# Windowed attention and two MLPs: sixteen attention items with the exponential taken after the transpose and a turned value product, and zero products on TensorE

## The chip, the cores and the metric

One NeuronCore of a Trainium2 chip runs the whole program as one launch. The metric is the device time of that core in microseconds (us), median over runs. TensorE is PE in the profile's rows, VectorE DVE, ScalarE ACT, GpSimd POOL; SP issues the DMAs.

## What is computed

Attention over 4 batches, 8 heads, 576 positions and head size 64, with a window of 128 keys and a linear bias per head, then two MLPs (512 to 2048 to 512) on the 2304 tokens. The weights arrive as 8-byte floats. Cut to what matters:

```python
scores = scale * q @ k.T + bias          # bias = -slope[h] * |i - j|
scores = where((rel >= 0) & (rel < 128), scores, -1e9)
attn = exp(scores - max(scores))
attn = attn / (sum(attn) + 1e-09)
x = (attn @ v)                           # heads side by side: 2304 x 512
h = x @ w_in;  x = (max(h, 0) + alpha * min(h, 0)) @ w_out
h = x @ moe2_w_in;  out = (h * sigmoid(1.702 * h)) @ moe2_w_out
```

## The kernel before

An attention *item* is one (unit, batch, head). Unit 0 holds queries 0 to 255, unit 1 queries 256 to 575; there are 64 items, unit 0 first. The first 16 (`n < FP`: batches 0 and 1 of unit 0) work in plain float32; the later ones split every operand into two float32r halves. Only the first 16 change.

Such a float32 item goes through these stages, each a function that is called with the item's number: `a_qk` (TensorE, L342: scores of two chunks, 128 and 256 keys), `a_bias` (VectorE, L362: scores plus bias, negated, into `tt`, and the row minimum into `st`), `a_exp` (ScalarE, L378: two exponentials in place with the row sum, each with a read of its accumulator), `a_recip` (VectorE, L386 and L387), `a_norm` (VectorE, L398, two), `a_trans` (TensorE, L411: three 128x128 transposes into PSUM), `a_pt_hi` (ScalarE, L418: copy of 384 columns into `pt`), `a_av` (TensorE, L432: the padded values `vz` as weights, `pt` streaming 256 and 128 columns; two heads share one tile `x`), and for each odd head `a_x3` (ScalarE L479 and VectorE L107: `xh` and `xl`, the two halves of the first MLP's input). GpSimd lays the values into `vz` (L328).

Ten *rounds* of a preamble (L741 to L776) run items 0 to 9 and decode weights beside them; then come the steps of the first MLP. A step is one of 16 slices `f` of the hidden size for one block `k` of 256 tokens: `m1_h` (L493, 12 products), `m1_n` (ScalarE L508), `m1_g` (VectorE L518, ScalarE L522), `m1_lo` (VectorE), and two steps later `m1_o` (L544, 12 products). Two steps carry one attention item. Block 0 needs items 0 to 7, and its 16 steps also decode the rest of the 32 chunks of the first MLP's weights. Each 512 KB chunk takes `w_scale` (ScalarE L147 and L150), `w_shift` and `w_add` (VectorE L154 and L159) and `w_split` (ScalarE L102, VectorE L107; for two early chunks VectorE L103). At most four chunks are in flight (`wstage`).

A scheduler sets the order of each engine's queue before the launch; engines then take their queue strictly in that order. The decode's instructions are pinned in program order, the others move. PSUM tiles of attention share four buffers (`ps_a`); the first MLP's accumulators are `o0` and `o1`.

Of the kernel before, what the change touches and what calls it, by code (L numbers as in the profile page):

```python
# [21 lines left out]
P = 128  # L22
# [43 lines left out]
def tile_window_attention__then__two_mlps(  # L66
# [255 lines left out]
    @stage  # L322
    def a_split_v(n, b, u, h, U):
        nv = (2, 4)[u]
        vr = raw_of(n)[:, UCOLS[u] - nv * D : UCOLS[u]].rearrange("p (j d) -> p j d", d=D)
        if n < FP:
            d0 = (h % 2) * D
            nc.gpsimd.tensor_copy(vzs[n % 2][:, :, d0 : d0 + D], vr)  # L328
# [43 lines left out]

    @stage
    def a_exp(n, b, u, h, U):
        tt, s = tts[n % 2], sts[n % 2]
        for i, (c0, rows, kk, keys) in enumerate(U["chunks"]):
            t = tt[:rows, i * 256 : i * 256 + keys]
            nc.scalar.activation(  # L378
                t, t, AF.Exp, bias=s[:rows, i : i + 1], scale=-1.0, accum_out=s[:rows, 4 + i : 5 + i]
            )  # L380

    @stage
    def a_recip(n, b, u, h, U):
        s = sts[n % 2]
        m = len(U["chunks"])
        nc.vector.tensor_scalar(s[:, 8 : 8 + m], s[:, 4 : 4 + m], 1e-9, None, op0=ALU.add)  # L386
        nc.vector.reciprocal(s[:, 12 : 12 + m], s[:, 8 : 8 + m])  # L387

    @stage
    def a_norm(n, b, u, h, U, eng):  # L390
        tt, s = tts[n % 2], sts[n % 2]
        for i, (c0, rows, kk, keys) in enumerate(U["chunks"]):
# [8 lines left out]
    def a_trans(n, b, u, h, U):  # L401
        tt = tts[n % 2]
        banks = [ps_a.tile([P, 512], F32, tag="a", name="pt") for _ in range(1 + u)]
        for i, (c0, rows, kk, keys) in enumerate(U["chunks"]):
# [9 lines left out]
    @stage  # L414
    def a_pt_hi(n, b, u, h, U, i):
        if i <= u:
            x, c, w = st["t", n][i]
            nc.scalar.copy(pts[n % 2] if n < FP else ar["pth"][:, c : c + w], x[:, :w])  # L418

# [5 lines left out]

    @stage
    def a_av(n, b, u, h, U):
# [40 lines left out]
    def a_x3(n, b, u, h, U):  # L468
# [3 lines left out]
        if n < FP:  # L472
            xp = st["x", n]
        t = u * B * UNITS[0]["nq"] + b * nq
# [232 lines left out]
    for t in vzs:  # L707
        nc.gpsimd.memset(t, 0.0)
    for t in sts:
# [26 lines left out]
    for t in tts:  # L736
        nc.gpsimd.memset(t[:, 512:768], 0.0)
    W1 = 2 * NF
    a_qk(0)
    w_ahead()  # L740
    for n in range(H + 2):  # L741

        if n == 4:
            nc.sync.dma_start(out=relt, in_=rel)
            nc.sync.dma_start(out=alph, in_=alpha)
            nc.gpsimd.tensor_scalar(beta, alph, -1.0, 1.0, op0=ALU.mult, op1=ALU.add)
        a_av(n - 2)
        a_split_v(n)
# [29 lines left out]
    a_split(n)  # L778
    for i in range(2):
        a_pt_lo(n - 2, i)  # L780
    a_recip(n - 1)
    a_norm(n - 1, "dve")
    a_av(n - 2)
    a_x1(n - 2)
    a_x2(n - 2)
    a_x3(n - 2)
    at0.close()
# [4 lines left out]
    for s, (k, f) in enumerate(steps):  # L792
# [14 lines left out]
        m1_h(k, f)  # L807
        if s % 2 == 0:
            a_trans(m)
            a_qk(n)  # L810
            a_pt_hi(m, 0)
            m1_n(k, f)
            m1_g(k, f)
            a_pt_hi(m, 1)
            a_bias(n)
            wd("shift")
            a_pt_lo(m, 0)
# [6 lines left out]
        else:  # L824
            a_av(m)
            if n == FP:
                a_parts()
# [11 lines left out]
            m1_lo(k, f, "dve")  # L839
            a_x3(n - 1)  # L840
        if k == 0:
# [136 lines left out]
```

## Time and profile before

| what | value |
|---|---|
| time, median of 3 runs | 948.61 us (948.21 to 950.05) |
| the profiled execution's own time | 951.22 us |
| its span, first to last instruction | 949.4 us |
| busy: PE, DVE, ACT | 926.7, 687.6, 526.7 us |

A row of groups names line, engine, operation, tiles, shape and count, then busy time and the mean of one; a row of the timeline gives start, length and engine, and how long the engine was idle before it and for what. A matmul's shown length contains its latency; the pitch of a stream is the distance of two starts. "x4" for two float32 products is right: each runs as two instructions.

### The profile page before, as it was taken

The numbers are of one execution on the slowest core, as the hardware profiler recorded it, in microseconds if no ns is written. First come the engines' busy times: TensorE is split into PE (matmuls) and PEld (weight loads), VectorE is DVE, ScalarE is ACT, GpSimd is POOL, SyncE is SP. The second block draws the span as 40 slices with busy tenths as digits, with TensorE's granted clock in tenths as the row PEclk, the third lists the DMA queues.
The fourth block names the chain that finished last, engine by engine and source line by source line (L and its number), as shares of the span: only waits on it lengthen the run. The fifth ranks groups of instructions, "written<-read, shape, count | busy, mean of one in ns | idle before, by whom it ended". The sixth has DMA issues, their size and how long they took to land.

```text
span 949.4 us, 17872 instructions
## 1 busy us (share of the span) xinstructions
PE 926.7 (98%) x6536; PEld 862.2 (91%) x6536; DVE 687.6 (72%) x1743; ACT 526.7 (55%) x1325; POOL 89.7 (9%) x127
## 2 busy tenths in 40 slices
PE   6899999999999999999999999999999999999997
PEld 3698899999999999999988888888898899999997
DVE  6898876778888888888457753685333798878876
ACT  5999866667667676676344443564232553433333
POOL 1100211122222222222000000000000000000000
PEclk9999999999999999999999999999999999999999
DMA  9666511223222222221023344665332333433323
GB/s 242 205 217 209 183 54 55 66 68 91 69 67 91 67 68 91 67 90 44 1 89 110 112 128 169 203 227 199 117 124 99 134 134 117 151 133 132 132 72 112
DMA packets 44041, 112.45 MB, mean 118 GB/s; under 512 B 5041, under 2 KB 15153, under 8 KB 43953
## 3 DMA queue, kind: packets, MB, share of 16 engines
q1 hardware_dynamic: 43952, 111.31, 36.1%
q8 instruction: 51, 0.84, 0.4%
q14 instruction: 38, 0.30, 0.1%
HBM read 82.98 MB, written 28.31 MB: 117 GB/s over the span
## 4 chain that ended last, share of the span: by engine, by line
PE 91%; DVE 2%; issue 1%; ACT 0%; DVEq 0%; ACTq 0%
PE h L493 21%; PE h L591 21%; PE p L658 18%; PE o L544 17%; PE p L544 5%; PE x L444 3%; PE pt L411 3%; PE s L351 1%; PE s L352 1%; PE s L342 1%; DVE wl L107 0%; DVE wd L159 0%; ACT oh L102 0%; PE x L432 0%; DVE wd L154 0%
## 5 line engine op out<-in xcount | busy, mean ns | idle before, releaser
L493 PE MATMUL h<-xh,wh 128*128 128x256 f32 (+1 forms) x512 | 151.9, 298 | 1.4 <-ACT xh L479 1.4
L493 PE MATMUL h<-xh,wl 128*128 128x256 f32 (+1 forms) x512 | 152.3, 298 | 0.0
L493 PE MATMUL h<-xl,wh 128*128 128x256 f32 (+1 forms) x512 | 151.4, 296 | 0.0
L658 PE MATMUL p<-wh,oh 128*128 128x256 f32 x504 | 136.3, 284 | 1.0 <-ACT oh L102 0.6
L658 PE MATMUL p<-wl,oh 128*128 128x256 f32 x504 | 136.2, 283 | 0.0
L544 PE MATMUL o<-gh,wl 128*128 128x256 f32 x448 | 127.5, 286 | 0.0
L544 PE MATMUL o<-gh,wh 128*128 128x256 f32 x448 | 125.9, 286 | 0.7 <-ACT gh L522 0.7
L544 PE MATMUL o<-gl,wh 128*128 128x256 f32 x448 | 125.5, 281 | 1.1 <-DVE gl L107 1.1
L658 PE MATMUL p<-wh,ol 128*128 128x256 f32 x504 | 119.2, 283 | 0.4 <-DVE ol L107 0.4
L591 PE MATMUL h<-x2h,wh 128*128 128x512 f32 (+1 forms) x320 | 117.9, 368 | 0.0
L591 PE MATMUL h<-x2l,wh 128*128 128x512 f32 (+1 forms) x320 | 117.8, 368 | 0.0
L591 PE MATMUL h<-x2h,wl 128*128 128x512 f32 (+1 forms) x320 | 117.7, 368 | 0.0
L605 DVE TENSOR_TENSOR g<-h,sg 128x512 f32<-128x512 f32 (+1 forms) x80 | 51.0, 638 | 90.7 <-ACT sg L601 90.5
L601 ACT ACTIVATE sg<-h 128x512 f32<-128x512 f32 (+1 forms) x80 | 44.4, 555 | 108.5 <-PE h L591 108.3
L493 PEld LDWEIGHTS h<-xh,wh 128*128 128x128 f32 x512 | 96.3, 189 | 5.2 <-ACT xh L479 1.9
L493 PEld LDWEIGHTS h<-xh,wl 128*128 128x128 f32 x512 | 96.6, 189 | 3.9 <-DVE wl L107 0.6
L493 PEld LDWEIGHTS h<-xl,wh 128*128 128x128 f32 x512 | 97.0, 189 | 3.0 <-issue 0.3
L658 PEld LDWEIGHTS p<-wh,oh 128*128 128x128 f32 x504 | 96.5, 192 | 2.1 <-ACT oh L102 2.0
L658 PEld LDWEIGHTS p<-wl,oh 128*128 128x128 f32 x504 | 96.7, 192 | 0.1
L518 DVE SCALAR_TENSOR_TENSOR g<-n,beta,h 128x256 f32<-128x256 f32 x112 | 53.2, 475 | 54.1 <-ACT n L508 53.8
L508 ACT ACTIVATE n<-h 128x256 f32<-128x256 f32 x112 | 42.8, 383 | 87.8 <-PE h L493 87.3
L658 PEld LDWEIGHTS p<-wh,ol 128*128 128x128 f32 x504 | 86.5, 192 | 0.7 <-DVE ol L107 0.6
(105 smaller groups left out, 2203.0 us busy)
## 6 DMA issues: line engine op xcount, KB each, us to landing
ws<-in_w_in_dram SPq DMA_DIRECT2D x32, 512.0 KB, 3.9
ws<-in_w_out_dram SPq DMA_DIRECT2D x32, 512.0 KB, 3.7
raw<-in_u_dram SPq DMA_DIRECT2D x32, 512.0 KB, 3.5
g2d<-g SPq DMA_DIRECT2D x32, 512.0 KB, 3.1
gr<-g2d SPq DMA_DIRECT2D x32, 512.0 KB, 3.2
raw<-in_u_dram SPq DMA_DIRECT2D x16, 320.0 KB, 2.8
wd<-x2d SPq DMA_DIRECT2D x36, 128.0 KB, 2.9
out_dram<-ob SPq DMA_DIRECT2D x16, 256.0 KB, 3.4
```

The costliest lines, as they stand in the source:

```text
L342: nc.tensor.matmul(o[:, :keys], raw[:, c0 : c0 + rows], raw[:, 256 + kk : 256 + kk + keys], start=True, stop=True)
L351: nc.tensor.matmul(o[:, :n_], q, kh[:, ks : ks + n_], start=True, stop=False)
L411: nc.tensor.transpose(banks[bank][:, dst : dst + P], src, ident)
L444: nc.tensor.matmul(x[:, oc : oc + nq], v, p[:, col : col + nq], start=(i == 0 and k == 0), stop=(i == len(js) - 1 and k == 1), skip_group_ ...
L493: nc.tensor.matmul(ph, w[:, 0, c * P : (c + 1) * P], x[:, c, r : r + n], start=(c == 0 and i == 0), stop=(c == NC - 1 and i == 2),)
L508: nc.scalar.activation(n, ph, AF.Relu, scale=-1.0)
L518: nc.vector.scalar_tensor_tensor(g, n, beta[:, f : f + 1], ph, op0=ALU.mult, op1=ALU.add)
L544: nc.tensor.matmul(o, w[:, 1, c * P : (c + 1) * P], g, start=(f == 0 and (k == KM or c % 2 == 0) and i == 0), stop=(f == NF - 1 and i == 2 ...
L591: nc.tensor.matmul(ph[:, :n], w[:, f % 2, c * P : (c + 1) * P], x[:, c, :n], start=(c == 0 and i == 0), stop=(c == NC - 1 and i == 2),)
L601: nc.scalar.activation(sg[:, :n], ph[:, :n], AF.Sigmoid, scale=1.702)
L605: nc.vector.tensor_tensor(g[:, f % 2, :n], ph[:, :n], sg[:, :n], op=ALU.mult)
L658: nc.tensor.matmul(o[:, m, :], g[:, a, m * P : (m + 1) * P], w, start=(p == 0 and m == 0 and i == 0), stop=(p == NF // 2 - 1 and i == 2), ...
```

## The change

For items 0 to 15 the exponential, its row sum and the division move. `f_sub` turns `tt` into score minus maximum (chunk 0 on VectorE, chunk 1 on ScalarE). `a_trans` then transposes those differences, and `f_exp` takes one exponential of 384 columns from PSUM into `pt`, where the plain copy was. `f_av` turns the product round: 128 columns of `pt` are the weights and the values stream, 64 columns and a column of ones, which yields the row sum; three products of 65 columns instead of two of 256 and 128. `f_div` divides once for two heads (three VectorE instructions), and `a_x3` transposes the result back (two transposes for two heads). `a_exp`, `a_recip`, `a_norm`, `a_pt_hi` and `a_av` do nothing for these items any more. An item's tail runs a round earlier (`a_x3(n - 1)` for `a_x3(n - 2)`).

From round 2 on each preamble round issues five products of a zero tile by itself (bfloat16, 128x128 by 128x512) into `o1`, three after `f_av` and two after the transposes: 40 in all. Their result is overwritten later.

```diff
-    vzs = [apf.tile([P, 2, P], F32, name=f"vz{i}") for i in range(2)]
+    vzs = [apf.tile([P, 2, D + 1], F32, name=f"vz{i}") for i in range(2)]
+    xq = apf.tile([P, 2, 2, D], F32, name="xq")
...
+    def f_sub(n, b, u, h, U):
...
+            if i:
+                nc.scalar.activation(t, t, AF.Identity, bias=s[:rows, i : i + 1], scale=-1.0)
+            else:
+                nc.vector.tensor_scalar(t, t, s[:rows, i : i + 1], -1.0, op0=ALU.subtract, op1=ALU.mult)
...
+    def f_exp(n, b, u, h, U):
+        if n < FP:
+            x, c, w = st["t", n][0]
+            nc.scalar.activation(pts[n % 2], x[:, :w], AF.Exp)
...
+    def f_av(n, b, u, h, U):
...
+        for c, j, col in ((0, 0, 0), (1, 0, 128), (1, 1, 256)):
+            nc.tensor.matmul(
+                x[:, c, h % 2, : D + 1], pt[:, col : col + P], vz[:, j, :],
+                start=(c == j == h % 2 == 0), stop=(c == j), skip_group_check=True,
+            )
...
+    def f_div(n, b, u, h, U):
...
+        nc.vector.tensor_scalar(r, x[:, :, :, D], 1e-9, None, op0=ALU.add)
+        nc.vector.reciprocal(f, r)
+        nc.vector.tensor_tensor(xq, x[:, :, :, :D], f.unsqueeze(3).to_broadcast([P, 2, 2, D]), op=ALU.mult)
...
     def a_av(n, b, u, h, U):
         if n < FP:
-            x = st["x", n] = st["x", n - 1] if h % 2 else ps_a.tile([P, 512], F32, tag="a", name="x")
-            pt, vz = pts[n % 2], vzs[n % 2]
-            for j in range(2):
-                nc.tensor.matmul(
-                    x[:, j * P : 256], vz[:, j, :], pt[:, j * 256 : 256 + j * P],
-                    start=(h % 2 == 0 and j == 0), stop=(h % 2 == 1 and j == 1), skip_group_check=True,
-                )
             return
...
         if n < FP:
-            xp = st["x", n]
+            xp = ps_a.tile([P, 512], F32, tag="a", name="x")
+            for i in range(2):
+                nc.tensor.transpose(xp[:, i * P : (i + 1) * P], xq[:, i, :, :], ident)
...
+    idle = pso.tile([P, 2, T1], F32, tag="o1", name="idle")
+    zero = tts[0][:, 512:768].bitcast(BF16)
+
+    def busy(m):
+        for _ in range(m):
+            tc.keep_in_program_order(nc.tensor.matmul(idle, zero[:, :P], zero, start=True, stop=True))
...
-        a_av(n - 2)
+        f_exp(n - 1)
         a_split_v(n)
...
         a_bias(n)
+        f_sub(n)
         w("split")
-        a_exp(n)
-        a_recip(n - 1)
+        f_av(n - 1)
+        busy(3 if n > 1 else 0)
         w("shift")
-        a_norm(n - 1, "dve")
-        a_trans(n - 1)
         w("add")
         w_ahead()
+        f_div(n - 1)
+        a_trans(n, True)
+        busy(2 if n > 1 else 0)
         w("scale")
-        a_x3(n - 2)
         if n % 4 == 0:
             w("split")
             w("shift")
-        a_pt_hi(n - 1, 0)
-        a_pt_hi(n - 1, 1)
+        a_x3(n - 1)
```

TensorE's queue in the preamble, before, from the scores of item 4 on (`h` is a first piece of `m1_h`):

```order
L342 MATMUL s<-raw_144 128x128
L342 MATMUL s<-raw_144 128x256
L432 MATMUL x<-pt_161,vz_159 128x256
L432 MATMUL x<-pt_161,vz_159 128x128
L411 MATMUL pt<-ident,tt_146 128x128 x3
L493 MATMUL h<-xh,wh_223 128x256
L493 MATMUL h<-xh,wh_286 128x256
```

The same place after the change; the last two rows come three times in a row there, and twice more behind the next transposes. Ahead of this piece stand the turned product of item 1 and five such products:

```order
L518 MATMUL x<-ident,xq 128x128 x2
L342 MATMUL s<-raw_144 128x128
L342 MATMUL s<-raw_144 128x256
L461 MATMUL xq<-vz_158,pt_161 128x65 x3
L789 LDWEIGHTS tt_146
L789 MATMUL idle<-tt_146 128x512
```

The transposes back (L518) stand in front of the scores of item 4, so these wait for the division of items 0 and 1; the turned product of item 2 stands right behind the scores.

ScalarE's queue around the exponential of item 3, before:

```order
L418 COPY pt_161<-pt 128x384
L378 ACTIVATE tt_147,st_149<-tt_147,st_149 128x128
L378 ACTIVATE tt_147,st_149<-tt_147,st_149 128x256
L147 ACTIVATE wd<-ws 128x512
L150 ACTIVATE ws<-ws 128x512
L479 CAST xh<-x 128x256
```

And after:

```order
L389 ACTIVATE pt_161<-pt 128x384
L381 ACTIVATE tt_147<-tt_147,st_149 128x256
L147 ACTIVATE wd<-ws 128x512
L150 ACTIVATE ws<-ws 128x512
L524 CAST xh<-x 128x256
L381 ACTIVATE tt_146<-tt_146,st_148 128x256
```

Two exponentials with a sum have become one subtraction, the copy has become the exponential, and the decode of a chunk stands between them as before. Up to the first `n` of block 0, 13 chunks are scaled on ScalarE and 11 items have their bias on VectorE in either order; up to the 24th `g` it is all 32 chunks and 22 items in either.

## Rows read from the trace of the kernel before

**Rows 1.** The page's second part: 40 slices of 23.7 us, busy tenths and granted clock.
```profile
PE   6899999999999999999999999999999999999997
...
PEclk9999999999999999999999999999999999999999
```

**Rows 2.** Windows: stretch, length; busy (count) of PE, PEld, DVE, ACT, POOL; clock; DMA.
```profile
0.00:49.00 49.00, 35.99 (x135) 25.04 (x136) 35.70 (x126) 35.70 (x92) 7.22 (x24) 1.00 0.81 227
49.00:107.00 58.00, 55.43 (x410) 50.03 (x410) 53.81 (x152) 53.23 (x137) 4.92 (x11) 1.00 0.68 215
107.00:150.00 43.00, 43.00 (x370) 43.00 (x369) 31.38 (x103) 28.64 (x91) 8.45 (x14) 1.00 0.22 72
```

**Rows 3.** Timeline of TensorE: scores of items 2, 4 and 7.
```profile
10.83 1.65 PE L342 MATMUL s<-rawf 64*128 64x128 f32 x4 [1.75 <-DMA rawf<-in_u_dram]
...
18.93 1.65 PE L342 MATMUL s<-raw 64*128 64x128 f32 x4
...
32.92 0.92 PE L342 MATMUL s<-rawf 64*128 64x128 f32 x4
```

**Rows 4.** Timeline of TensorE and its weight loads, 34 to 50 us.
```profile
34.11 0.49 PE L411 MATMUL pt<-ident,tt 128*128 128x128 f32 x3
...
46.86 0.52 PEld L342 LDWEIGHTS s<-raw 64*128 64x128 f32 x4
...
46.86 0.92 PE L342 MATMUL s<-raw 64*128 64x128 f32 x4
47.71 0.44 PE L411 MATMUL pt<-ident,tt 128*128 128x128 f32 x2
...
48.86 0.89 PE L432 MATMUL x<-pt,vz 128*128 128x256 f32 x4
49.70 0.39 PE L493 MATMUL h<-xh,wh 128*128 128x256 f32 x1
```

**Rows 5.** The chain that ended last, in order of time: start, time on it, what.
```profile
54.37 2.60 PE o L544 x22
...
58.04 0.65 PE x L432 x4
...
93.54 0.46 DVE tt L398 x2
```

**Rows 6.** Windows, line L591 alone (128x512 products): PE busy (count), PEld busy, clock.
```profile
600.00:650.00 50.00, 50.00 (x222) 41.43 (x221) 1.00 0.61 211
```

**Rows 7.** Groups of VectorE by form, 31 to 105 us.
```profile
L398 DVE TENSOR_SCALAR tt<-tt,st 128x256 f32<-128x256 f32 x12 | 4.4, 363 | 0.0
...
L398 DVE TENSOR_SCALAR tt<-tt,st 128x128 f32<-128x128 f32 x12 | 3.6, 302 | 0.1
L107 DVE TENSOR_TENSOR xl<-x,xh 128x256 fp32r<-128x256 f32 x7 | 2.9, 416 | 0.1
...
L386 DVE TENSOR_SCALAR st<-st 128x2 f32<-128x2 f32 x12 | 2.1, 177 | 0.6 <-ACT tt L378 0.6
L387 DVE RECIPROCAL st<-st 128x2 f32<-128x2 f32 x12 | 1.9, 160 | 0.2
```

**Rows 8.** Groups of ScalarE by form, 31 to 105 us.
```profile
L378 ACT ACTIVATE tt<-tt,st 128x256 f32<-128x256 f32 x12 | 6.1, 505 | 0.0
...
L418 ACT COPY pt<-pt 128x384 f32<-128x384 f32 x12 | 5.7, 477 | 3.0 <-PE pt L411 2.9
...
L378 ACT ACTIVATE tt<-tt,st 128x128 f32<-128x128 f32 x12 | 4.9, 405 | 0.0
L378 ACT ACTIVATION_READ_ACCUMULATOR tt<-tt,st 128x1 f32 x23 | 4.5, 196 | 0.0
...
L315 ACT ACTIVATE q<-raw 128x256 fp32r<-128x256 f32 x2 | 0.9, 432 | 0.0
```

**Rows 9.** Timelines of ScalarE and VectorE: the first `n` and the fifteenth `g` of block 0.
```profile
48.66 0.39 ACT L508 ACTIVATE n<-h 128x256 f32<-128x256 f32 x1
...
106.19 0.47 DVE L518 SCALAR_TENSOR_TENSOR g<-n,beta,h 128x256 f32<-128x256 f32 x1
```

More of the change, by code (lines that the diff above doesn't have):

```diff
@@ L373, in a_exp @@
     @stage
+    def f_sub(n, b, u, h, U):
+        if n >= FP:
+            return
+        tt, s = tts[n % 2], sts[n % 2]
+        for i, (c0, rows, kk, keys) in enumerate(U["chunks"]):
+            t = tt[:rows, i * 256 : i * 256 + keys]
+            if i:
+                nc.scalar.activation(t, t, AF.Identity, bias=s[:rows, i : i + 1], scale=-1.0)
+            else:
+                nc.vector.tensor_scalar(t, t, s[:rows, i : i + 1], -1.0, op0=ALU.subtract, op1=ALU.mult)
+    @stage
+    def f_exp(n, b, u, h, U):
+        if n < FP:
+            x, c, w = st["t", n][0]
+            nc.scalar.activation(pts[n % 2], x[:, :w], AF.Exp)
+    @stage
     def a_exp(n, b, u, h, U):
         tt, s = tts[n % 2], sts[n % 2]
+        if n < FP:
+            return
         for i, (c0, rows, kk, keys) in enumerate(U["chunks"]):
@@ L385, in a_recip @@
         m = len(U["chunks"])
+        if n < FP:
+            return
         nc.vector.tensor_scalar(s[:, 8 : 8 + m], s[:, 4 : 4 + m], 1e-9, None, op0=ALU.add)
@@ L391, in a_norm @@
         tt, s = tts[n % 2], sts[n % 2]
-        for i, (c0, rows, kk, keys) in enumerate(U["chunks"]):
+        for i, (c0, rows, kk, keys) in enumerate(U["chunks"] if n >= FP else ()):
             t = tt[:rows, i * 256 : i * 256 + keys]
@@ L400, in a_trans @@
     @stage
-    def a_trans(n, b, u, h, U):
+    def a_trans(n, b, u, h, U, fp=False):
         tt = tts[n % 2]
+        if (n < FP) != fp:
+            return
         banks = [ps_a.tile([P, 512], F32, tag="a", name="pt") for _ in range(1 + u)]
@@ L415, in a_pt_hi @@
     def a_pt_hi(n, b, u, h, U, i):
-        if i <= u:
+        if i <= u and n >= FP:
             x, c, w = st["t", n][i]
-            nc.scalar.copy(pts[n % 2] if n < FP else ar["pth"][:, c : c + w], x[:, :w])
+            nc.scalar.copy(ar["pth"][:, c : c + w], x[:, :w])
     @stage
@@ L426, in a_av @@
     @stage
+    def f_av(n, b, u, h, U):
+        if n >= FP:
+            return
+        if h % 2 == 0:
+            st["xq", n // 2] = (pso if n < H else ps_a).tile(
+                [P, 2, T1], F32, tag="o0" if n < H else "a", name="xq"
+            ).rearrange("p c (h t) -> p c h t", h=2)
+        x = st["xq", n // 2]
+        pt, vz = pts[n % 2], vzs[n % 2]
+        for c, j, col in ((0, 0, 0), (1, 0, 128), (1, 1, 256)):
[3 more added lines that the diff above has]
+            )
+    @stage
+    def f_div(n, b, u, h, U):
+        if n >= FP or h % 2 == 0:
+            return
+        s, x = sts[n % 2], st["xq", n // 2]
+        r, f = (s[:, i : i + 4].rearrange("p (c h) -> p c h", c=2) for i in (8, 12))
+        nc.vector.tensor_scalar(r, x[:, :, :, D], 1e-9, None, op0=ALU.add)
+        nc.vector.reciprocal(f, r)
+        nc.vector.tensor_tensor(xq, x[:, :, :, :D], f.unsqueeze(3).to_broadcast([P, 2, 2, D]), op=ALU.mult)
+    @stage
     def a_av(n, b, u, h, U):
         if n < FP:
-            x = st["x", n] = st["x", n - 1] if h % 2 else ps_a.tile([P, 512], F32, tag="a", name="x")
-            pt, vz = pts[n % 2], vzs[n % 2]
-            for j in range(2):
-                nc.tensor.matmul(
-                    x[:, j * P : 256], vz[:, j, :], pt[:, j * 256 : 256 + j * P],
-                    start=(h % 2 == 0 and j == 0), stop=(h % 2 == 1 and j == 1), skip_group_check=True,
-                )
             return
@@ L778, in tile_window_attention__then__two_mlps @@
     a_split(n)
[L779 to L786, printed above, removed]
+    f_exp(n - 1)
     at0.close()
@@ L808, in tile_window_attention__then__two_mlps @@
         if s % 2 == 0:
+            f_av(m)
             a_trans(m)
@@ L814, in tile_window_attention__then__two_mlps @@
             a_pt_hi(m, 1)
+            f_div(m)
             a_bias(n)
+            f_sub(n)
             wd("shift")
@@ L825, in tile_window_attention__then__two_mlps @@
             a_av(m)
+            a_trans(n, True)
+            f_exp(n)
+            if m < FP:
+                a_x3(m)
             if n == FP:
@@ L839, in tile_window_attention__then__two_mlps @@
             m1_lo(k, f, "dve")
-            a_x3(n - 1)
+            if m >= FP:
+                a_x3(m)
         if k == 0:
```

5 lines of the change are left out of this document (2 added, 3 removed).

## The prediction

> **What bounds the kernel now.** I read the slices first: TensorE is busy 6 and 8 tenths in the first two and 9 or more in nearly all that follow [rows 1]. The windows say the same by stage: from 107 us on PE is busy all the time and VectorE 31.4 of 43 us, so from there the time is TensorE's own work, which the change does not touch [rows 2]. What can be won or lost lies ahead of that. There are two stages. Stage one runs to the first `n` of block 0 at 48.66 us [rows 9]: PE is busy 36.0 of 49 us, VectorE and ScalarE 35.7 each, and DMA has a share of 0.81, so nothing is saturated alone [rows 2]. Stage two ends about where the fifteenth `g` starts at 106.19 us [rows 9]: PE 55.4, VectorE 53.8 and ScalarE 53.2 of 58 us [rows 2], all nearly full; its chain runs over TensorE first and from about 88 us over VectorE, where the normalization L398 itself stands on it [rows 5].
>
> Then I read single rows of TensorE. The same four instructions of an item's scores take 1.65 us at 10.83 and 18.93, and 0.92 us at 32.92 [rows 3]. [...] So in stage one TensorE works at half speed for two thirds of the time, and this is what the zero products address.
>
> **Prices.** At the higher level: a set of scores 0.85 us, from 46.86 to the next start at 47.71 [rows 4]. Three transposes show 0.49 us with their latency [rows 4]; I take 0.45. A product `a_av` took 0.65 us on the chain [rows 5] and 0.84 from 48.86 to 49.70 where it stood alone [rows 4]. A float32r product of 256 columns is 2.60 us / 22 = 0.118 [rows 5]. A zero product streams 512 columns; the nearest row is L591, 50.0 / 222 = 0.225 [rows 6]. At the lower level I double.
>
> The turned product `f_av` is not in the trace: three products are six instructions, each with a load of 128 float32 columns and a stream of 65. Four such loads took 0.52 us together [rows 4], 0.13 each, so 6 x 0.13 = 0.78 us where the load sets the pace. The low end is 0.65, the old product; the high end adds the stream, a quarter of a 256-column instruction's (0.65 / 3 = 0.22 [rows 5]), to each load: 6 x 0.185 = 1.1. I take 0.78, since in `a_av` the loads vanished behind the streams. [...]
>
> **Stage one, TensorE.** Both kernels start the scores of item 2 at 10.83 us, when its data land [rows 3]. After the change the queue then holds, at the lower level: two sets of scores (2 x 1.6), the transposes of items 1 and 2 (2 x 0.85), two `f_av` (2 x 1.56), five zero products (5 x 0.45 = 2.25) and two transposes back (0.45), 10.7 in all: the scores of item 4 start at 21.5 us, where they started at 18.93 before [rows 3]. I let the clock rise there: TensorE has then worked without a stop through `f_av` and five full products.
>
> From there a pair of rounds holds two sets of scores 1.70, six transposes 0.90, two `f_av` 1.56, ten zero products 2.25, two transposes back 0.35, and six pieces of `h` 0.80: 7.56, and 0.2 for the wait of L518 on `f_div` that the products don't cover: 7.75 us. Three pairs give 23.25. The last round then adds `f_av` 0.78, five products 1.13, transposes 0.45, scores 0.85 and `h` 0.80: 4.0. So the first `n` comes at 21.5 + 23.25 + 4.0 + 0.2 = 48.95, **+0.3 us** against 48.66 [rows 9].
>
> The other engines don't hold this up. ScalarE loses two exponentials, two reads and a copy, 0.405 + 0.505 + 2 x 0.196 + 0.477 = 1.78 us an item, and gains a subtraction of 256 columns (between 0.432, L315, and 0.505; I take 0.5) and an exponential of 384 columns out of PSUM (between the copy's 0.477 and 0.605, the L378 forms carried on; 0.55): -0.73 [rows 8]. VectorE loses 0.177 + 0.160 + 0.302 + 0.363 = 1.00 and gains 0.302 for `f_sub` and half of `f_div`, (0.177 + 0.160 + 0.416) / 2 = 0.38: -0.32 an item [rows 7]. Both had 13 us of idle time in stage one [rows 2]. On GpSimd the copy of the values keeps its size and its buffer comes free a round earlier; the loads on SP keep their order but for a place or two. These go together at nothing, covered by the same idle time; if it were gone, a chunk's landing would hold ScalarE's queue, and with it the exponentials behind it.
>
> **Stage two.** Per engine, between the first and the 24th `g` both orders hold the same 20 or so chunks and 11 items. The normalization of items 10 to 15 goes (6 x 1.00) and five `f_sub` (1.5) and four `f_div` (3.0) come: VectorE -1.5 us. TensorE gains four pairs of transposes back, 4 x 0.35 = +1.4. Where VectorE sets the pace the end is -1.5, where TensorE does it is +1.4. I take **-0.9**: VectorE and not TensorE stands on the chain in the later half, with L398 among it [rows 5].
>
> **Sum.** +0.3 - 0.9 = -0.6 us. Against the profiled execution's own 951.22 us that is 950.6; that execution lies 2.6 us over the median, so for the median 948.61 - 0.6 = **948.0 us**. A measurement of this kernel can tell about 0.2%, 1.9 us, from no change, so this forecast is no change.
>
> **Rivals.**
> *The products cost nothing and the clock rises with them (faster).* Where VectorE and ScalarE still set the rounds, the zeros lie in waits. Before, three pairs took 46.86 - 18.93 = 27.9 us, 9.3 each [rows 3, 4]; 1.5 us less ScalarE work a pair gives 7.8, and with `f_av` at 0.65 and the waits gone TensorE needs 7.3, 0.45 less than I took. With the clock rising at the first of the five products (-1.1) and stage two at -1.5: 0.3 - 1.1 - 3 x 0.45 - 1.5 = -3.65, 945.0. For it: 13 us of idle on each engine in stage one. Against it: ten products a pair are the largest term of TensorE's pair. 0.38.
>
> *Zeros do not raise the clock, or late (slower; the change then does not do what it is written for).* [...] A pair is then 2 x 7.4 less little, some 14 us. If the level rises at some 32.5 us as now, the 11 us from 21.5 cover 0.8 of a pair instead of 1.42: +4.9 us, 952.9. For it: TensorE was at work well before 32 us without a rise [rows 1, 3]. Against it: those streams were scores of 64 rows and transposes, with gaps; the products are full and back to back. 0.18; of it 0.04 that it stays low through all of stage one, +18 us, which I leave out of the range.
>
> *The loads of `f_av` do not overlap (slower).* 6 x 0.185 = 1.1 us: 0.32 x 9 + 0.64 x 2 = +4.2 in stage one, of which I count 3.5, the rest lying in waits: 951.5. The two prices of `a_av` above speak against it. 0.06.
>
> *Attention runs ahead in stage two (slower).* Items from 16 on are heavier for VectorE, and the new order puts more of them in front of the end of the decode; each brings its normalization again, 1.00 us of VectorE [rows 7], and its bias. If TensorE starves for one and a half of them: +1.5 and more, 950 to 951. 0.04.
>
> **How the numbers follow.** Forecast 0.34 (its own range 946.7 to 950.5), the faster rival 0.38 spread over 943 to 946.7, the slower ones 0.28. The likeliest value stays that of the sum, since the faster rival has no single price. The range leaves out a tenth on each side: 942.5 to 953.5. Faster 0.38, same 0.34, slower 0.28.
>
> **What would show it.** In the profile of the changed kernel: the scores of item 4 near 21.5 us, and their length (0.92 or 1.65 us) for the clock; pairs of rounds near 7.7 us; six instructions of `f_av` within 0.8 to 0.9 us, zero products at 0.225; the first `n` near 49 us; the wait of L518 on the division under 0.3 us; ScalarE idle in stage one up by some 7 us. The prediction is wrong if the first `n` moves by more than 2 us either way, or if PE is full before 100 us.

## The result, and the profile after

The changed kernel takes **956.52 us** (median of 8 runs, 954.04 to 961.53) against 950.40 us (8 runs of the kernel before on the same chip, 948.21 to 952.98). The ratio is **1.0067, 95% interval 1.0043 to 1.0091**: slower by two thirds of a per cent. The forecast was 948.0 us and no change; the time lies outside the range, which ended at 953.5. The profiled execution took 956.78 us, with a span of 955.0 us; before it was 951.22 and 949.4. All that follows is about these 5.6 us of span. (Two executions further down took far longer, one of `no_zeros` with 1833.26 us at a mean granted clock of 1.000 and one of the kernel before with 1440.05 us at 0.589; both are left out of the ratios.)

The windows of the two stages, changed kernel, to be laid beside [rows 2] (stretch, length; busy and count of PE, PEld, DVE, ACT, POOL; granted clock; DMA share, GB/s):

```profile
0.00:49.00 49.00, 41.70 (x206) 27.54 (x206) 32.80 (x109) 32.51 (x64) 5.89 (x24) 0.97 0.75 224
49.00:107.00 58.00, 54.53 (x407) 50.06 (x406) 52.62 (x144) 49.20 (x115) 7.07 (x13) 0.97 0.64 201
107.00:150.00 43.00, 40.96 (x340) 40.19 (x341) 29.81 (x90) 26.70 (x81) 7.03 (x10) 1.00 0.26 86
```

In stage one TensorE does 5.7 us more, and VectorE and ScalarE some 3 us less each, as the change intends. Before, PE was busy all the time from 107 us on; now 2.0 us are missing there. The timeline of the changed kernel shows where stage two ends (start, length, engine, line, what):

```profile
49.22 0.86 DVE L563 SCALAR_TENSOR_TENSOR g<-n,beta,h 128x256 f32<-128x256 f32 x2
...
112.39 0.69 DVE L159 CUSTOM_DVE_ANT_0 wd<-ws,wd 128x1024 uint16<-128x1024 uint16 x1
...
114.05 0.47 DVE L563 SCALAR_TENSOR_TENSOR g<-n,beta,h 128x256 f32<-128x256 f32 x1
```

The first `g` comes at 49.22 us, before it was 49.16: **stage one came out even**. The fifteenth `g` comes at 114.05 against 106.19 [rows 9]. The row between them is VectorE's addition for the 32nd weight chunk, the last that block 0 decodes. It ends at 113.08; before, the same addition ran from 106.58 to 107.26. The two rows of the kernel before:

```profile
49.16 0.48 DVE L518 SCALAR_TENSOR_TENSOR g<-n,beta,h 128x256 f32<-128x256 f32 x1 [0.21 <-ACT n L508]
...
106.58 0.68 DVE L159 CUSTOM_DVE_ANT_0 wd<-ws,wd 128x1024 uint16<-128x1024 uint16 x1
```

This end is the best single reading of this kernel: in the profiles of 19 kernels (before, after, and all below but `no_zeros`) it lay between 104.6 and 114.0 us, and the span ended 841.0 to 844.1 us after it every time. So what delays VectorE's 32nd chunk delays the whole, but for some 3 us that it does not explain.

That end can be taken apart, as VectorE's work ahead of it plus VectorE's idle time. First the changed kernel, then the kernel before, in windows that end with the 32nd chunk:

```profile
0.00:50.00 50.00, 42.56 (x211) 28.11 (x212) 33.80 (x111) 33.51 (x65) 6.19 (x25) 0.97 0.75 223
50.00:75.00 25.00, 25.00 (x201) 23.70 (x201) 22.84 (x64) 21.64 (x49) 1.45 (x3) 1.00 0.69 211
75.00:113.08 38.08, 33.05 (x232) 29.40 (x230) 34.68 (x94) 32.34 (x81) 6.78 (x11) 0.96 0.62 202
```

```profile
0.00:50.00 50.00, 36.99 (x140) 25.86 (x141) 36.53 (x128) 36.70 (x96) 7.34 (x25) 1.00 0.81 229
50.00:75.00 25.00, 25.00 (x191) 22.84 (x190) 22.76 (x66) 22.26 (x56) 1.04 (x3) 1.00 0.56 175
75.00:107.26 32.26, 29.69 (x219) 26.64 (x219) 30.48 (x87) 30.23 (x79) 3.76 (x8) 1.00 0.75 240
```

DVE column: up to 75 us the change saves 36.53 + 22.76 - 33.80 - 22.84 = 2.65 us of work, and all of it turns into idle time (16.2 against 13.5 us in the first 50). Behind 75 us VectorE does 34.68 instead of 30.48, **4.2 us more**, and is idle 3.4 instead of 1.8 us. Together: -2.65 + 4.2 + 2.7 + 1.6 = 5.85, of 113.08 - 107.26 = 5.82. Taken over all three windows, VectorE's work is 1.55 us more and its idle time 4.27 us more. The groups of VectorE behind 75 us show the work, changed kernel first, then before (count | busy us, mean ns | idle before):

```profile
L159 DVE CUSTOM_DVE_ANT_0 wd<-ws,wd 128x1024 uint16<-128x1024 uint16 x11 | 8.8, 796 | 0.2
...
L318 DVE SCALAR_TENSOR_TENSOR q<-raw,q 64x256 fp32r<-64x256 f32 x4 | 2.9, 726 | 0.1
...
L362 DVE CUSTOM_DVE_ANT_0 tt<-s,relt 128x256 f32<-128x256 f32 x3 | 1.2, 414 | 0.0
L107 DVE TENSOR_TENSOR ptl<-pt,pth 128x384 fp32r<-128x384 f32 x2 | 1.1, 544 | 0.0
...
L508 DVE TENSOR_TENSOR xp<-x,tb 64x256 f32<-64x256 f32 x2 | 0.8, 412 | 0.0
```

```profile
L159 DVE CUSTOM_DVE_ANT_0 wd<-ws,wd 128x1024 uint16<-128x1024 uint16 x12 | 8.1, 683 | 0.1
...
L317 DVE SCALAR_TENSOR_TENSOR q<-raw,q 64x256 fp32r<-64x256 f32 x2 | 0.8, 424 | 0.1
L362 DVE CUSTOM_DVE_ANT_0 tt<-s,relt 128x256 f32<-128x256 f32 x2 | 0.8, 416 | 0.0
...
L107 DVE TENSOR_TENSOR ptl<-pt,pth 128x384 fp32r<-128x384 f32 x1 | 0.5, 543 | 0.0
```

Items from 16 on (`relt`, `q`, `ptl`, `xp`) are the float32r ones. One or two more of each stage of them stand ahead of the last chunk: by VectorE's timeline 19 items have their bias ahead of the 32nd chunk and of the fifteenth `g`, where the kernel before has 18, and four `q` stand there where it has two. And `q` and the addition L159 are longer than before, which the last section takes up.

Two things more are new on TensorE in this profile. It waits for the division, and its clock falls (rows of its timeline, then windows inside two stretches, where the granted clock is the third figure from the right):

```profile
19.70 0.92 PE L342 MATMUL s<-raw 64*128 64x128 f32 x4
20.55 0.88 PE L461 MATMUL xq<-vz,pt 128*128 128x65 f32 x6
21.27 0.81 PE L789 MATMUL idle<-tt 128*128 128x512 bf16 x3
...
26.84 0.92 PE L342 MATMUL s<-rawf 64*128 64x128 f32 x4
...
35.02 0.44 PE L518 MATMUL x<-ident,xq 128*128 128x128 f32 x2 [1.27 <-DVE xq L474]
35.39 0.92 PE L342 MATMUL s<-raw 64*128 64x128 f32 x4
...
100.03 0.39 PE L538 MATMUL h<-xh,wh 128*128 128x256 f32 x1 [1.44 <-ACT wh L102]
```

```profile
37.00:40.00 3.00, 3.00 (x11) 1.53 (x10) 2.15 (x5) 2.25 (x5) 0.33 (x1) 0.50 0.53 149
...
101.50:104.50 3.00, 3.00 (x16) 3.00 (x15) 2.57 (x9) 2.92 (x8) 0.59 (x1) 0.50 0.63 205
```

The granted clock stood at 0.50 from 36.6 to 40.0 and from 101.4 to 104.9 us. A zero product took 0.43 us there (three from 37.29 to 38.57) and 0.21 at 1.00 (three from 21.27 to 21.91), a product of 256 columns 0.21 (102.02 to 102.23) and 0.12 (24.08 to 24.20). Ahead of the second fall the wait was not for the division: TensorE waited 1.44 us, up to 100.03, for ScalarE's half of a weight chunk (`wh`).

The rise ahead of that is read from lengths alone. The granted clock is 1.00 from 0 to 36 us in both profiles, but the same scores take 1.65 us up to 28.26 in the kernel before and 0.92 from 32.92 on [rows 3], in the changed kernel 1.65 up to 13.55 and 0.92 from 19.70 on. These two speeds are the lower and the higher level of the prediction. "The clock rose" stands below for the time of this change; that it is the clock is the author's reading.

The profile of the kernel before shows no fall, once the clock had risen, but that execution is not the usual one. Every execution on record has its mean granted clock, and one stretch of 3.4 us at 0.50 lowers that mean by about 0.0018 (3.41 / 2 / 955). The profiled one has 0.999. Of the 113 executions of the kernel before beside the experiments, 77 have 0.995 or 0.996, about as low as the changed kernel's profile (0.995), and so must hold at least one such stretch by this estimate, beside a stretch at 0.50 at the very end (some 2 us in the profile of the kernel before, 3.3 us in that of the changed one). Their median is 949.1 us; the 21 at 0.999 have 950.6. So in the kernel before falls of the clock are usual, and executions with them are no slower; `before_hold`, below, shows one of 6.8 us from 37.3 us in an execution of 948.39 us. In the changed kernel the three executions at 0.997 took 954.0 to 955.2 us and the five at 0.995 took 956.3 to 961.5.

### The profile page after: what moved, and what is told of

It reads as the page before. It is cut to its first block, busy times and chain, and to the rows that moved or that the text cites. A ratio compares the mean times of both kernels' runs of the same rounds, so it can differ in the third digit from the quotient of the medians.

```text
span 955.0 us, 17953 instructions
## 1 busy us (share of the span) xinstructions
PE 935.1 (98%) x6624; PEld 867.5 (91%) x6624; DVE 685.6 (72%) x1719; ACT 521.0 (55%) x1277; POOL 90.1 (9%) x127
## 4 chain that ended last, share of the span: by engine, by line
PE 86%; DVE 2%; ACT 1%; issue 1%; DVEq 0%; ACTq 0%
PE h L636 20%; PE h L538 19%; PE p L703 18%; PE o L589 15%; PE p L589 5%; PE x L487 3%; PE pt L435 3%; PE s L351 1%; PE s L352 1%; ACT oh L102 0%; DVE wl L107 0%; DVE gs L677 0%; DVE ol L107 0%; DVE wd L159 0%; DVE g L650 0%
```

## The experiments

Three theories were set against each other: the zero products cost TensorE's time; the float32r items that run ahead cost VectorE's; the clock that falls costs TensorE's (A, B and C in the first expectations are the items, the products and the clock). Ratios are against runs of the kernel before on the same chip in the same hour. None of these kernels leaves part of the computation out.

**The products alone, without them, and fewer of them.** `zeros_alone`: the kernel before with

```
+        busy(3 if n > 1 else 0)      # behind a_av(n - 2)
+        busy(2 if n > 1 else 0)      # behind a_trans(n - 1)
```

> The kernel before with the 40 zero products alone (three behind the value product, two behind the transposes of each round from the third on); its order behind 50 us stays that of before. Theory A: the time moves only by what stage one moves: the clock rises at about 20 us instead of 32, TensorE gets 9 us more work, ScalarE and VectorE bound the later rounds as before, so -2 to +2 us against the kernel before, 947 to 952. Theory B: 954 to 957, nearly all of the loss.

951.41 us, ratio 1.0006 (0.9991 to 1.0021): no change. The clock rose at 25.2 us against 32.5 (one profile each), the first `g` came at 49.0. In the kernel before, the products neither cost nor give anything by themselves.

`no_zeros`: the changed kernel with `busy(0)` in both places.

> The changed kernel without its 40 zero products. Theory A: what matters is the order behind 84 us, which here puts three and not four of the heavier items in front of the decode's end; stage one loses the early clock (first g at 51 to 54 us instead of 49.2) but not the products' 9 us of TensorE, and the whole lies between 951 and 957. Theory B: 950 or below, the first g not later than 49.2. [...]

962.0 us (median of four), 1.0127 (1.0107 to 1.0148), which neither theory had. The rewrite needs them: without them it is twice as far behind. Why is not shown.

`zeros_early_rounds`: `1 < n < 5` in place of `n > 1`, 15 products instead of 40.

> The changed kernel with the zero products in the third to fifth round only, 15 instead of 40. [...] Its order behind 84 us is nearly that of the change (four heavier items in front), so theory A expects 953 to 957 all the same; theory B 950 to 952.

956.21 us, 1.0062 (1.0046 to 1.0079). That is the number of the items' theory. The first `g` came 2.1 us earlier, at 47.1, but the clock was at 0.5 from 43.2 to 50.0 and twice more in stage two, and the 32nd chunk ended at 111.1. What stage one won was gone by then.

**The order in block 0.** `hold_items`: the changed kernel with the float32r items' biases kept in program order; 17 items then have theirs ahead of the 32nd chunk.

```
-            nc.vector.tensor_tensor_reduce(
+            ins = nc.vector.tensor_tensor_reduce(
...
+            if n >= FP:
+                pin(ins)
```

> The changed kernel, with only the bias of the float32r items (17th item on) pinned behind the weight decode on VectorE; up to the 16 float32 items nothing moves, all 40 zero products stay. Theory A (the loss arose between 84 and 115 us, because VectorE's new order puts four of the heavier items in front of the end of the decode, where the kernel before has two): the 32nd w_add, 112.4 us after the change and 106.6 before, comes back to 105 to 108 us, the time falls by 4 to 6 us to about 950. Theory B (the zero products cost it): no gain, 955 to 957. Theory C (the two stretches of 3.4 us at half the clock cost it): the one at 36 us stays, the one at 101 us may go, so 1 to 2 us at most.

954.65 us, 1.0056 (1.0034 to 1.0078). Its windows:

```profile
75.00:109.87 34.87, 31.50 (x224) 29.20 (x223) 30.62 (x77) 28.32 (x65) 4.06 (x8) 0.90 0.66 210
```

VectorE's work behind 75 us is back at the 30.5 us of before, as the theory has it, but its idle time rose to 4.2 us and the 32nd chunk still ended at 109.9, not at 105 to 108. VectorE's waits there end with ScalarE's half of a weight chunk (1.9 us) and with TensorE's scores and turned product (1.6 us). TensorE itself waits too, by its timeline, and then runs at a granted clock of 0.50, with 0.21 us an instruction (5.52 / 26) where it has 0.11 from 106.5 to 112 us (5.50 / 49):

```profile
97.86 0.44 PE L520 MATMUL x<-ident,xq 128*128 128x128 f32 x2 [1.40 <-DVE xq L476]
99.29 0.58 PE L540 MATMUL h<-xh,wh 128*128 128x256 f32 x1 [0.99 <-ACT wh L102]
```

```profile
99.50:105.50 6.00, 5.52 (x26) 5.23 (x26) 5.12 (x14) 5.63 (x16) 1.12 (x2) 0.50 0.71 231
```

Two waits, the first for the division, and behind them 6.8 us at 0.50, 3.4 us of TensorE's work by the author's estimate (half of 6.8). On the changed kernel, then, the pin alone gains 0.11%, well inside the intervals: waits took the place of the work.

**The wait and the clock.** `x3_late`: `hold_items` with the transposes back of items 11 and 13 where the float32r items have them.

```
-            if m < FP:
-                a_x3(m)
             if n == FP:
+                a_x3(m)
                 a_parts()
...
             m1_lo(k, f, "dve")
-            if m >= FP:
+            if n != FP:
                 a_x3(m)
```

> hold_items with the transposes back and the copies of the finished pair (x3) of items 11 and 13 moved to the end of the odd step, where heavy items have them. In hold_items TensorE waited 1.40 us for the division at 97.86 and the clock fell at 99.2. If that wait is what lets the clock fall: the wait is gone or under 0.5 us, no stretch at 0.5 between 80 and 120 us, total 951 to 952. Rival, the clock falls from the sum of small waits and weaker work in block 0: another wait takes its place, a stretch at 0.5 remains, total 954 to 955.

952.02 us, **1.0020** (1.0007 to 1.0034). In its profile TensorE did not wait 0.9 us or more for the division in block 0, there was no stretch at 0.5, and VectorE was idle behind 75 us 1.9 instead of 4.2 us (TensorE did wait 1.63 us for weights at 100.5, with no fall behind it):

```profile
75.00:110.12 35.12, 32.08 (x248) 29.42 (x247) 33.24 (x87) 31.71 (x72) 5.76 (x9) 1.00 0.70 223
```

This execution took longest, 955.47 us (there the first `g` came as late as 53.3), and isn't the usual one either. By mean granted clock, four of the 12 executions are at 0.998 and took 949.4 to 950.4 us, level with the kernel before; six are at 0.995 or 0.996, so with falls that the profile doesn't have, and took 951.6 to 953.1; the profiled one and one more are at 1.000 and took 955.5 and 953.5. So the edit removed the falls in some executions only, and the median is one of those that have them.

`hold_fill`: `hold_items` with eight products ahead of `h` in steps 8 to 14, `matmul(ph, pw[:, 0, :P], pw[:, 0, :n])` with `pw` the weights of the step before; the real product overwrites them.

> hold_items with eight more products of 256 columns (a weight tile times itself, 0.118 us each, overwritten by the real product) ahead of the h of steps 8 to 14 of block 0; they do not depend on the step's own weights. If the clock is the larger part of the loss: no stretch at 0.5 between 80 and 120 us, the 6.8 us at half rate (3.4 us of work) come back, fifteenth g near 107, total 950 to 951.5 against 954.65 of hold_items. Rival, the work and its order on VectorE set stage two and the clock only follows: 7 x 8 x 0.118 = 6.6 us more on TensorE, of which the part outside waits is lost, 956 or more.

952.73 us, 1.0034 (1.0023 to 1.0046). Its profile has no fall of the clock from its rise to 946 us (four of the ten executions, at 0.996 or 0.997, must have had one), and 6.6 us of added products did no harm. The gain on `hold_items` is about half of what was expected, and the intervals of the two overlap.

`div_early`: `x3_late` with `f_div(n - 1)` ahead of `w("shift")` in the preamble.

> x3_late with the division of the preamble moved ahead of the round's decode on VectorE. In the changed kernel TensorE waited 1.27 us for the division at 35.02 and the clock fell at 36.6. If the wait lets it fall: no stretch at 0.5 between 20 and 80 us, first g at 47 to 48 (half of 3.4 us back), total 1 to 2 us below x3_late. Rival, VectorE now stands waiting for TensorE's products and the decode comes late by as much: first g at 49.5 or later, total as x3_late or above.

951.52 us, 1.0028 (1.0015 to 1.0040). The wait of 1.27 us went and the first `g` came at 46.0, 3 us ahead of the changed kernel's, more than expected; but the total is that of `x3_late`. In block 0 the wait for the division was back, 1.41 us at 95.19 us, and the clock at 0.50 from 98.8 to 102.2.

`x3_late_free`: the edit of `x3_late` on the changed kernel, order left free.

> The changed kernel with the transposes back of items 11 and 13 at the end of the odd step, and nothing held in order (the biases of heavy items as free as in the changed kernel). Of the 5.8 us by which VectorE ends its 32nd chunk later (113.1 against 107.3), its idle time behind 75 us has 1.6 (3.4 against 1.8), items run ahead the larger part of the rest. If TensorE's wait for the division in block 0 is a cause by itself: idle behind 75 us about 2, no stretch at 0.5 between 80 and 120 us, total 953 to 954, 0.2% or more under the changed kernel. If the items ahead are the cause and the wait only goes with them: total 955 or more.

953.99 us, 1.0043 (1.0027 to 1.0058): the first theory's number, but not its signs. In the profile (its longest execution, 958.10 us) a wait for the division came back, 1.71 us at 100.65 us, and the clock fell at 110.2. The edit also moves VectorE's order: three `q` and one `ptl` instead of four and two stand ahead of the 32nd chunk, so it does not isolate the wait. With `hold_items` this gives a square: changed kernel 1.0067, order held 1.0056, x3 late 1.0043, both 1.0020. Both together give 0.47%, the two alone 0.11 and 0.24; the intervals are too wide to say that they help each other.

**Where the loss lies.** `old_in_block`: the rewrite for items 0 to 9 only (`NW = H + 2` in place of `FP` in the new and the switched stages); items 10 to 15, in block 0, as before.

> The rewrite is kept for items 0 to 9 (all of the preamble, zeros included) and items 10 to 15, which lie in block 0, are computed as before; VectorE's order in block 0 is then the one of before. If the loss is made by the rewritten items inside block 0 (order and clock there): first g near 49.2 as after, granted clock 1.0 between 80 and 120 us, fifteenth g near 106, total within 0.15% of before. Rival, the rewritten preamble leaves the loss behind (its clock fall near 37 us, late loads): the fifteenth g still at 110 or later and the total 0.4% or more above before.

952.50 us, 1.0031 (1.0018 to 1.0044). Over half of the loss goes: the six rewritten items in block 0 make it, with the order and the waits that they bring, which this run does not part. The rest is neither theory's number; the 32nd chunk ended at 108.5 after 17.1 us of idle time ahead of 50 us.

`old_block_div`: the same with the early division. `old_block_div_hold`: that with the biases pinned as above.

> old_in_block with the preamble's division ahead of the round's decode on VectorE (as in div_early, without its other edits). old_in_block has VectorE idle for 17.1 us ahead of 50 us, 3.6 more than the kernel before, although its rewritten items give it less to do. If it is TensorE's waits for the division that leave it idle: first g at 46 to 47, that idle time 14.5, total 949.5 to 951. Rival, the share is the clock's spread and nothing that an order mends: total 952 to 953 as old_in_block. The earlier division also shifts block 0 (19 items ahead of the fifteenth g where old_in_block has 18), which may take back 1 us.

> old_block_div with the biases of heavy items held in program order (17 items ahead of the fifteenth g). If items running ahead cost something by themselves: 1 us or more under old_block_div, 948.5 to 950, level with before. Rival, the decode's own rate sets the end: as old_block_div.

955.40 us, 1.0050 (1.0033 to 1.0067), slower than either theory had, and 951.57 us, **1.0019** (1.0009 to 1.0029), more than the 1 us gained but not level with before. This is the cleanest pair: it differs in the pin alone (19 and 17 items ahead of the 32nd chunk), the intervals lie apart, 3.8 us between the medians. Windows behind 75 us, free and held:

```profile
75.00:112.00 37.00, 32.91 (x218) 29.02 (x217) 36.34 (x101) 34.76 (x89) 7.19 (x11) 0.91 0.70 225
```

```profile
75.00:107.25 32.25, 27.84 (x202) 24.53 (x202) 31.49 (x80) 29.40 (x72) 5.48 (x8) 1.00 0.71 236
```

VectorE is idle 0.7 and 0.8 us in them, and has 4.85 us more to do ahead of the 32nd chunk where the order is free. Of these, 1.7 us are work that the free one had not done by 75 us (its first `g` came at 48.7 in its profile, the other's at 46.9). The other 3.2 us are what runs ahead, and come back in the total. The free one's profile also has the clock at 0.50 for 6.8 us from 103.8, the other's none; but VectorE stood idle for only 0.7 us there, so the fall did not hold its 32nd chunk up. Nor is it the clock alone by single executions: at a mean granted clock of 0.994 to 0.996 the six of the free order took 952.7 to 955.8 us, four of the held one 951.8 to 953.0. **In this pair, items that run ahead of the decode's end are paid for.**

`old_block_few_zeros`: `old_block_div` with `busy(2)` and `busy(1)`.

> old_block_div with three zero products a round instead of five (two and one). If the zeros lie on TensorE's path in the preamble: 16 x 0.225 = 3.6 us less work, first g 1 to 3 us earlier than old_block_div, unless the clock falls more. If they only fill waits: first g the same; if they are what holds the clock: more time at 0.5 between 20 and 50 us and first g later.

954.58 us, 1.0050 (1.0035 to 1.0065), first `g` at 46.5, 2.2 us earlier, as expected of products on TensorE's path. But the total is that of `old_block_div`: the products' own time is not the loss. Nine of the 12 executions have a mean granted clock of 0.999 or 1.000, which by the estimate above leaves no room for a fall of 3.4 us, and they took 950.2 to 957.2 us; so it is not falls of the clock alone either.

**An earlier clock.** `early_zeros`: the changed kernel with nine products more, where TensorE waits for the first data.

```
+    busy(2)
     a_qk(0)
     w_ahead()
     for n in range(H + 2):
+        busy((4, 3)[n] if n < 2 else 0)
```

> The changed kernel with nine zero products more, in the gaps in which TensorE waits for the first data: two ahead of the scores of item 0, four behind those of item 1 and three behind those of item 2. In five profiles of the same preamble the clock rose at 18.3, 19.5, 20.6, 20.7 and 31.6 us and the first g came at 47.3 to 53.3: that spread would be the preamble's share of the loss, some 0.2 to 0.3% by old_in_block. If so: rise by 15 us, first g at 46 to 47, total 953 to 954.5 against 956.52. Rival, the rise is not the preamble's matter (its data and the decode are): first g 49 and the total as the changed kernel's.

955.27 us, 1.0051 (1.0038 to 1.0063). The clock rose at 11.1 us, the first `g` came at 47.4; the total is a little lower than the changed kernel's, within the intervals.

`before_early`: the nine products in the kernel before.

> The kernel before, without the rewrite, with the nine zero products of early_zeros alone. If a risen clock is worth something by itself in stage one: rise by 15 us against 32.5, first g 1 us or more ahead of 49.2, total 948 to 949. Rival, as zeros_alone showed (rise at 25.2, first g 49.0, total the same): data and the two elementwise engines set stage one, total within 0.15% of before.

952.98 us, 1.0037 (1.0023 to 1.0051): slower, which neither theory had. In its profile the clock rose at 23.8 us and not by 15, and stood at 0.5 from 37.5 to 40.9 and from 44.3 to 51.2; the span was 949.5 us, no longer than that of before, but this was the shortest of its 12 executions. All 12 have a mean granted clock of 0.991 to 0.994, lower than any of the 113 of the kernel before, and the five longest (955.2 to 957.0 us) are at 0.991 or 0.992. So the higher median goes with longer falls; why the nine products bring them stays open.

`held_all` (`div_early`, six filling products a step, x3 one step later still) and `held_early` (with the nine products):

> div_early with six products more ahead of the h of steps 8 to 14 (as hold_fill, with six instead of eight) and the transposes back of items 11 and 13 behind the h of the next even step. If the clock and the wait for the division are what is left of the loss in block 0: no stretch at 0.5 from 20 to 140 us, fifteenth g at 105 to 106, span near 948.5, total 949.5 to 950.5. Rival, the fills cost what they give: as div_early, 951.5, or more.

> held_all with the nine zero products of early_zeros. If both shares add: first g at 44 to 45, total 1 to 2 us under held_all, 948 to 949 and with that level with before or below it. Rival, VectorE's decode sets the end of stage two whatever TensorE's clock does in the preamble: first g earlier, fifteenth g and total as held_all.

954.17 us, 1.0038 (1.0026 to 1.0050), and 958.57 us, 1.0098 (1.0078 to 1.0118). `held_all` shows no fall of the clock from 19.8 to 951 us and took 954.81 us all the same: VectorE's 32nd chunk ended at 112.0, TensorE still waited 1.25 us for the division at 99.19, VectorE was idle for 4.8 us behind 75 us. So a clock held up is not enough. Why `held_early` is the slowest was not found; its clock rose only at 21.1 us with the same nine products, its first `g` came at 49.7, and the clock fell at 38.2 and 103.0 behind waits of 1.27 and 1.26 us for the division.

**A better version.** `before_hold`: the kernel before with the pin. `zeros_hold`: `zeros_alone` with the pin.

> The kernel before with the biases of heavy items held in program order as in hold_items: 17 items ahead of the fifteenth g instead of 18. If VectorE's work ahead of its 32nd chunk sets the end of the decode and with it the time: busy 89.8 - 1 to 2 us, the 32nd chunk 1 to 2 us earlier, total 0.1 to 0.2% under before. Rival, the work let go is replaced by waits: total within 0.1% of before.

> zeros_alone (the kernel before with 40 zero products in the preamble) with the same order held. If the risen clock is worth something once VectorE's order does not eat it: a further 0.5 to 1 us under before_hold. Rival, as zeros_alone: the same as before_hold within 0.1%.

949.16 us, 1.0004 (0.9991 to 1.0017), and 951.37 us, 1.0013 (0.9997 to 1.0029). Nothing gained, and nothing tested of what counts: the pin takes one item from ahead of the fifteenth `g` (17 for 18), but ahead of the 32nd chunk both traces have the same 18, and VectorE's work up to it stayed at 89.9 us (89.8 before). No version beat the kernel before; the nearest with the rewrite are `old_block_div_hold` and `x3_late`, 0.2% behind.

## Why the prediction was wrong

- **Clock rise, scores of item 4 at 21.5 us: near.** 19.70 us, already 0.92 us long. That the zeros, or work without a stop, raise it is not shown: with the same preamble it rose in one profile at 31.6 us.
- **Prices: right.** `f_av` 0.78 was taken; its rows show 0.78 to 0.88 for six instructions, not the 1.1 of the high end. A zero product of 0.225: three from 21.27 to the transposes at 21.91, 0.21 each. That in `a_av` the loads vanished behind the streams shows in the kernel before, where four of its loads ran from 57.76 to 58.49 us and its products from 57.88, with the next product at 58.44. Doubling for the lower level was the author's estimate; in its place the changed kernel took 1.58 us for a set of scores (13.55 to 15.13), 1.18 for `f_av` (15.82 to 17.00) and 0.44 for a zero product (five from 17.00 to 19.19), where the prediction has 1.6, 1.56 and 0.45.
- **Pair of rounds 7.75 us: near on average.** 26.84 - 19.70 = 7.14, then 35.39 - 26.84 = 8.55, where the wait for the division was 1.27 us and not under 0.3. (The faster rival, held likelier than the forecast, put TensorE's pair at 7.3 us beside 7.8 for ScalarE; by its own figures ScalarE would have set the pair, and most of its gain was not there.)
- **Stage one +0.3 us: right on this profile within 1 us.** The first `n` came at 47.98, 0.7 us earlier than before, the first `g` 0.06 later. But it is one draw: the same preamble gave 47.3 (`hold_fill`), 49.7 (`hold_items`), 49.9 (`old_in_block`) and 53.3 (`x3_late`).
- **"These go together at nothing": right for stage one.** VectorE's saved time ahead of 75 us became idle time. ScalarE's work fell by 3.2 us up to 49 us (35.70 to 32.51), not by the 7 that were expected.
- **Stage two -0.9 us: the step that failed.** It counted work "between the first and the 24th `g`", where both orders hold as many items. The end of stage two is the decode's 32nd chunk, nine `g` earlier, and up to there the new order holds more float32r work: behind 75 us VectorE's work was +4.2, where the stage was to bring -1.5, and its idle time +1.6. Some 1.9 of the 4.2 are instructions that lasted longer beside GpSimd (last section), which no term had. Stage two's sum also let nothing but work count, and TensorE's waits for the division and the clock came on top. How the loss divides between these is not shown.
- **The rival "attention runs ahead" named one part of the mechanism, and was undervalued**: +1.5 us and a chance of 0.04. The pinned pair measures 3.8 us for two items, though on the changed kernel itself the same pin gained only 0.11%. Where the scheduler lays out the queue, what leaves VectorE's queue is replaced by whatever can come next, and here that was the dearer kind of item.
- **No rival had the clock fall again.** The prediction let it rise once and stay. Its share by itself isn't settled: executions of the changed kernel at 0.995 took 2.7 us longer than those at 0.997, and of `x3_late` at 0.995 or 0.996 2.4 us longer than those at 0.998 (medians); in the kernel before a lower mean went with no longer time; `held_all` and `old_block_few_zeros` show that without a fall in the profile the order and the waits can still cost 0.4 to 0.5%.
- **The prediction's own signs of being wrong did not come.** The first `n` moved by less than 2 us; the loss lay behind it, where no sign had been set.
- **Left open:** some 0.2% that every version with the rewritten preamble keeps, with VectorE idle 14 to 20 us ahead of 50 us. Earlier division, fewer zeros and more zeros moved the first `g` and not the total.

## What to carry to other kernels

Find the one event behind which the rest takes nearly the same time in every profile (here VectorE's 32nd chunk, 841 to 844 us from the end), and count work and idle time up to that event and not to a rounder one behind it. A change that frees an engine ahead of such an event brings nothing if the order lets dearer work of later stages slip in front of it: compare how much of each kind stands ahead of the event in both orders. Where a profile's clock rises or falls at another time in each execution, judge stages by several profiles, and see by the clocks of the other executions whether the profiled one is a usual one.

## What the runs showed of the hardware

**The clock fell behind waits of little over 1 us, in some profiles.** In three profiles with the same preamble (changed kernel, `hold_items`, `old_in_block`) TensorE waited 1.27 us for the division at 35.0 to 36.0 us, and the clock went to 0.5 for 3.4 us at 36.6 to 37.8. In `hold_fill` the same wait, at 34.8 us, had no such effect, nor in `x3_late`, at 40.7; and the kernel before, in its profile, waited 1.42 us at 39.1 and 1.10 us at 99.9 without a fall. So neither the wait nor the program alone decides. The rise moves as well, under the same preamble: in the changed kernel the scores of item 4 are already 0.92 us long at 19.70, in `x3_late` only those of item 6 are (its rows of items 4, 5 and 6):

```profile
20.12 1.65 PE L342 MATMUL s<-raw 64*128 64x128 f32 x4
25.94 1.65 PE L342 MATMUL s<-raw 64*128 64x128 f32 x4
32.55 0.92 PE L342 MATMUL s<-rawf 64*128 64x128 f32 x4
```

So the change of speed came at 19.7 us at the latest in one profile and behind 25.94 in the other. The fall at 101.4 us of the changed kernel came behind a wait of 1.44 us, up to 100.03.

**Some of VectorE's instructions were longer beside GpSimd.** Timelines of the changed kernel, VectorE and then GpSimd:

```profile
85.72 0.96 DVE L318 SCALAR_TENSOR_TENSOR q<-raw,q 64x256 fp32r<-64x256 f32 x1
...
93.36 1.22 DVE L159 CUSTOM_DVE_ANT_0 wd<-ws,wd 128x1024 uint16<-128x1024 uint16 x1
```

```profile
85.66 0.73 POOL L107 TENSOR_TENSOR kl<-raw,kh 128x256 fp32r<-128x256 f32 x1 [3.58 <-ACT kh L102]
...
93.00 1.03 POOL L107 TENSOR_TENSOR kl<-raw,kh 128x256 fp32r<-128x256 f32 x1 [6.61 <-DMA ws<-in_w_out_dram]
```

`q` takes 0.42 and L159 0.68 us where GpSimd is idle. Three `q` and three L159 behind 75 us began while a split of GpSimd was running, and are longer by 0.54 + 0.54 + 0.42 + 0.16 + 0.54 + 0.27 = 2.5 us; a `wl` adds 0.3. Not every instruction was longer: a split of `g` (L107) at 93.02 took 0.42 us beside GpSimd's split of 93.00, as others without it do. In the kernel before one L154 and two L398 are longer by 0.8 us in the same way, so the difference is about 1.9 of the 4.2 us. It is not what parts the pinned pair, whose two kernels have 1.8 and 2.0 us of it. In the kernel before a `q` met a split of the keys once in that stretch, and VectorE had begun first:

```profile
86.43 0.43 DVE L317 SCALAR_TENSOR_TENSOR q<-raw,q 64x256 fp32r<-64x256 f32 x1
```

```profile
86.53 0.93 POOL L107 TENSOR_TENSOR kl<-raw,kh 128x256 fp32r<-128x256 f32 x1
```

and there GpSimd was the longer one, with 0.93 us where the 14 later ones from 107.68 to 193.78 take 0.73 to 0.75. Why the lengths part like this is not shown. No run here took GpSimd's splits away, so what they cost in the total was not tried.
